# A GeGLU feed-forward kernel: ten blocks' first two products ahead instead of eight, x's first tokens loaded by halves of D, and two w_gate tiles kept in the result buffer

## The chip, the core and the metric

The kernel runs on one core of a Trainium2 chip. Five engines run their own instruction streams beside each other: TensorE (PE; its weight loads are PEld), VectorE (DVE), ScalarE (ACT), GpSimd (POOL) and SyncE (SP), which here only issues DMAs. The metric is the time of one execution on the device, in microseconds (us). A profile is one execution recorded by the hardware profiler; its span runs from the first to the last instruction of the program.

## The reference

`x` is 1024 tokens (32 x 32) by D = 1024, `w_gate` and `w_up` are 1024 x 3584, `w_down` is 3584 x 1024, all bf16.

```python
def _gelu(x):
    return jax.nn.gelu(x, approximate=True)

def reference(x, w_gate, w_up, w_down):
    return (_gelu(x @ w_gate) * (x @ w_up)) @ w_down
```

## The kernel before

Both stages are matrix products with one level of the Strassen-Winograd scheme: a product of 2 x 2 blocks is made with seven block products instead of eight, at the price of sums and differences of blocks. In the first stage the four blocks of the left side are the D halves of `w_gate` (a11 the first, a12 the second) and of `w_up` (a21, a22). The blocks of the right side are x transposed: B11 and B21 are the first and second D half of the first 512 tokens, B12 and B22 those of the other 512. The 3584 columns are cut into FT = 28 blocks of 128. One block product is four matmuls of 128 x 128 against 128 x 512, one for each 128 rows of a D half (KH = 4), accumulated in PSUM.

For each block i there are seven products. The first two, a11 x B11 and a12 x B21, are plain bf16 and need nothing but the loaded tiles (`first_products`, `second_products`; the matmuls are line 187). After the first, ScalarE copies the PSUM tile A to SBUF (E1, line 203); after the second it applies GELU to A (GL, line 210). The other five use sums: S1 to S4 of the weights, made by VectorE for blocks 0 and 1 and then by VectorE and GpSimd, and T1 to T4 of x, made once by VectorE (`t_sum`, line 158) from both halves of the tokens: T1 = B12 - B11, T2 = B22 - T1, T3 = B22 - B12, T4 = B21 - T2. `seed` (line 216) writes E1 back into PSUM as the start of a further sum.

The order of all instructions is written out by hand. The steps at the start are:

- Warm matmuls on a zeroed tile (line 137, NWARM = 18).
- SyncE issues the transposing DMA of x's first 512 tokens (xt0, line 135, 1 MB), then the pieces of the first w_gate tile (a tile holds two blocks' columns, 512 KB), tile 1, half of the first w_up tile, tiles 2 and 3, the transpose of the other 512 tokens (xt1, line 147), tile 4 and the rest of w_up. ScalarE issues one 128 KB piece of tile 0, after the fourth warm matmul.
- A lead of LEAD = 8 blocks: for each pair of blocks, two first products and two second products, 64 matmuls that need neither T1 to T4 nor S1 to S4.
- The further products of blocks 0 and 1, pairwise, mixed with the first products of blocks 8 and 9.
- A loop over i = 2 to 28 with the five further products of block i, and `ahead()`, which does the first product of the block `done` and the second of the one before. It is called in every iteration that is not in ALONE, until all blocks are done. A w_gate tile is loaded in every second iteration, into the one of five buffers (pool `gw`) that is free by then.

The four PSUM tiles that A and Y share (tag `q`) and the other four (tag `p`) are all of PSUM. E1 lies in a ring of four tiles, one for two blocks. The first stage's result goes to `gT` (28 blocks by 1024 tokens, bf16); the second stage multiplies it with `w_down` in the same scheme, and is left as it is.

Of the kernel before, what the change touches and what calls it, by code (L numbers as in the profile page):

```python
# [7 lines left out]
ACT = mybir.ActivationFunctionType  # L8
# [4 lines left out]
def kernel(  # L13
# [18 lines left out]
    nc = tc.nc  # L32
    P = nc.NUM_PARTITIONS
    fp32 = mybir.dt.float32
# [3 lines left out]
    xf = x.flatten_outer_dims()  # L38
    of = out.flatten_outer_dims()
    N, D = xf.shape  # L40
    F = w_gate.shape[1]
    NB = 512
    DT = D // P
    KH = DT // 2
    FT = F // P
# [1 line left out]
    DB = 512  # L47
    NDB = D // DB
    assert N == 2 * NB and DT % 2 == 0 and D % DB == 0 and FT % 4 == 0
    NWARM = 18  # L50
    LEAD = 8
    ALONE = (4, 7, 10, 13, 16, 19)
    KF = FT // 2
    TT = NT // 2
    JF = KF // 2
# [7 lines left out]
    ring = ctx.enter_context(tc.tile_pool(name="ring", bufs=RING))  # L63
# [2 lines left out]
    psum = ctx.enter_context(tc.tile_pool(name="ps", bufs=4, space=bass.MemoryType.PSUM))  # L66
    stage1 = ctx.enter_context(ExitStack())
    xpool = stage1.enter_context(tc.tile_pool(name="x", bufs=1))
    gw = stage1.enter_context(tc.tile_pool(name="gw", bufs=5))
    uw = stage1.enter_context(tc.tile_pool(name="uw", bufs=2))  # L70
    spool = stage1.enter_context(tc.tile_pool(name="s", bufs=2))
    epool = stage1.enter_context(tc.tile_pool(name="e", bufs=2))
# [1 line left out]
    gT = gpool.tile([P, FT, N], bf16, name="gT")  # L74
    xt0 = xpool.tile([P, DT, NB], bf16, name="xt0", tag="xt0")
    B11, B21 = xt0[:, :KH, :], xt0[:, KH:, :]
    xt1 = uw.tile([P, DT, NB], bf16, name="xt1", tag="uw")
    B12, B22 = xt1[:, :KH, :], xt1[:, KH:, :]
    WG, WU = {}, {}

    def load_gate(c, queue, lo=0, hi=DT):
        if c not in WG:
            WG[c] = gw.tile([P, DT, 2 * P], bf16, name="gw", tag="gw")
        queue.dma_start(
            out=WG[c][:, lo:hi, :], in_=wg_r[:, lo:hi, 2 * c * P : (2 * c + 2) * P]
        )

    def load_up(c, lo=0, hi=4):
        if c not in WU:
            WU[c] = uw.tile([P, DT, 4 * P], bf16, name="uw", tag="uw")  # L90
        nc.sync.dma_start(
            out=WU[c][:, :, lo * P : hi * P],
            in_=wu_r[:, :, (4 * c + lo) * P : (4 * c + hi) * P],
        )
# [4 lines left out]
    def a11(i):  # L99
        return block(WG, 2, i, 0)  # L100

    def a12(i):
        return block(WG, 2, i, 1)
# [4 lines left out]
    def a22(i):  # L108
        return block(WU, 4, i, 1)
# [12 lines left out]
    def psum_p(name):  # L122
        return psum.tile([P, NB], fp32, name=name, tag="p")

    def psum_q(name):
        return psum.tile([P, NB], fp32, name=name, tag="q")

    with tc.manual_schedule():
        zt = opool.tile([P, NB], bf16, name="zt", tag="o")
        nc.vector.memset(zt, 0.0)  # L130
        warm = [psum_p("warm") for _ in range(4)]
        table = opool.tile([P, 8], bf16, name="table", tag="o")
        nc.scalar.activation(table, zt[:, 0:8], ACT.Gelu_apprx_tanh)

        nc.sync.dma_start_transpose(out=xt0, in_=xf[0:NB, :])
        for n in range(NWARM):
            nc.tensor.matmul(warm[n % 4], lhsT=zt[:, 0:P], rhs=zt, start=True, stop=True)
            if n == 3:
                nc.scalar.activation(table, warm[n][:, 0:8], ACT.Copy)
                load_gate(0, nc.scalar, 0, 2)  # L140
        load_gate(0, nc.sync, 2, KH)
        load_gate(0, nc.sync, KH, DT)
        load_gate(1, nc.sync)
        load_up(0, 0, 2)
        load_gate(2, nc.sync)
        load_gate(3, nc.sync)
        nc.sync.dma_start_transpose(out=xt1, in_=xf[NB:N, :])
        load_gate(4, nc.sync)
        load_up(0, 2, 4)

        T = {}
# [3 lines left out]
        def t_sum(name, a, b, step=2):  # L155
            for k in range(0, KH, step):
                ks = slice(k, k + step)
                nc.vector.tensor_tensor(T[name][:, ks, :], a[:, ks, :], b[:, ks, :], ALU.subtract)
# [19 lines left out]
        def copy_a22(i):  # L178
            nc.scalar.activation(C22[i], a22(i), ACT.Copy)

        A, E1, GL = {}, {}, {}

        def pair_product(ps, lhs, rhs, first, cuts):
            for lo, hi in zip(cuts, cuts[1:]):
                for p, l in zip(ps, lhs):
                    for k in range(lo, hi):
                        nc.tensor.matmul(  # L187
                            p,
                            lhsT=l[:, k, :],
                            rhs=rhs[:, k, :],  # L190
                            start=(first and k == 0),
                            stop=(k == KH - 1),
                            skip_group_check=True,
                        )

        def first_products(*blocks, cuts=(0, KH)):
            for i in blocks:
                A[i] = psum_q("a")
            pair_product([A[i] for i in blocks], [a11(i) for i in blocks], B11, True, cuts)
            for i in blocks:  # L200
                if i % 2 == 0:
                    E1[i // 2] = ring.tile([P, 2, NB], fp32, name="e1", tag="ring")
                nc.scalar.activation(E1[i // 2][:, i % 2, :], A[i], ACT.Copy)  # L203

        def second_products(*blocks, cuts=(0, KH)):
            pair_product([A[i] for i in blocks], [a12(i) for i in blocks], B21, False, cuts)
            for i in blocks:
                if i % 2 == 0:
                    GL[i // 2] = half.tile([P, 2, NB], bf16, name="gl0", tag="half")
                nc.scalar.activation(GL[i // 2][:, i % 2, :], A[i], ACT.Gelu_apprx_tanh)  # L210
# [3 lines left out]
        def seed(i):  # L214
            X[i] = psum_p("x")
            nc.scalar.activation(X[i], E1[i // 2][:, i % 2, :], ACT.Copy)

        done = LEAD + 2

# [7 lines left out]
        def sixth_products(*blocks):  # L227
            cuts = range(0, KH + 1, 2)
            pair_product([X[i] for i in blocks], [S2[i] for i in blocks], T["T2"], False, cuts)
            for i in blocks:  # L230
                E2[i] = epool.tile([P, NB], fp32, name="e2", tag="e2")
                nc.scalar.activation(E2[i], X[i], ACT.Copy)
# [9 lines left out]
        def seventh_products(*blocks):  # L242
            cuts = range(0, KH + 1, 2)
            pair_product([X[i] for i in blocks], [S3[i] for i in blocks], T["T3"], False, cuts)
            for i in blocks:
                e3 = epool.tile([P, NB], fp32, name="e3", tag="e3")
                nc.scalar.activation(e3, X[i], ACT.Copy)  # L247
                U1[i] = epool.tile([P, NB], bf16, name="u1", tag="u1")
                nc.vector.tensor_tensor(U1[i], Y[i], e3, ALU.add)  # L249
# [16 lines left out]
        t_sum("T2", B22, T["T1"])  # L266
        t_sum("T3", B22, B12)
        t_sum("T4", B21, T["T2"])
        between = {2: lambda: copy_a22(0), 4: lambda: seed(0), 6: lambda: seed(1)}
        for n in range(0, LEAD, 2):  # L270
            first_products(n)
            first_products(n + 1)
            if n in between:
                between[n]()
            second_products(n)
            second_products(n + 1)
        for k in range(KH):
            nc.scalar.activation(T["B22"][:, k, :], B22[:, k, :], ACT.Copy)
        copy_a22(1)
# [2 lines left out]
        pair_product(  # L282
            [Y[0], Y[1]], [S1[0], S1[1]], T["T1"], True, range(KH + 1)
        )
        first_products(8)
        sixth_products(0, 1)
        first_products(9)
        seventh_products(0, 1)
        second_products(8)
        early_sums(2, nc.vector)  # L290
        second_sum(2)
        seed(2)
# [6 lines left out]
            third_product(i)  # L299
        copy_a22(2)  # L300
        finish(0)
        load_gate(5, nc.sync)
        load_up(1)

        for i in range(2, FT + 1):
            here, prev, more = i < FT, i - 1 if i > 2 else None, i + 1 < FT
            if more and i > 2:
                early_sums(i + 1)
            if here:
                sixth_products(i)  # L310
                if more:
                    seed(i + 1)
            if prev:
                fourth_product(prev)
            if more:
                second_sum(i + 1)
                late_sums(i + 1)
            if prev:
                finish(i - 2)
            if here:  # L320
                fifth_product(i)
            if here and i not in ALONE and done <= FT:
                ahead()
            if here:
                seventh_products(i)
                if more:
                    copy_a22(i + 1)
            if prev:
                third_product(prev)
            if here and i % 2 == 0:  # L330
                if i // 2 + 5 < FT // 2:
                    load_gate(i // 2 + 5, nc.sync)
                if i % 4 == 0 and i // 4 + 1 < FT // 4:
                    load_up(i // 4 + 1)
        finish(FT - 1)
# [37 lines left out]
        B11 = lambda j: V11[j // 2][:, two(j % 2), :]  # L373
        B12 = lambda j: V12[:, two(j), :]
        B21 = lambda j: V21[j]
# [149 lines left out]
```

## Time and profile before

| | |
|---|---|
| time, median of 3 runs | 277.34 us (276.94 to 277.44) |
| time of the profiled execution | 277.3 us |
| its span | 275.5 us |
| granted TensorE clock, mean | 1.000 |
| ACT busy | 137.9 us (50%) |
| read from HBM, written | 22.02 MB, 2.10 MB |

The times are us from the span's start. In the timeline a row gives the start, the length, the engine (SPq and ACTq are DMA issues), the line, the operation with output and inputs, the count of instructions merged into it, and in brackets the idle time before it and what ended it. The waits give who waited for whom, the total in us, how often, and the longest. Windows give for a stretch its length, then busy time and count of each engine, the granted clock, the DMA share and GB/s; with a line named, TensorE's matmuls and weight loads of that line alone. The DMA view of a stretch gives GB/s in 40 equal slices, the packets and bytes of the queues (q1 is SyncE's, q10 ScalarE's), and the DMAs issued in it with their size and the time from issue to landing.

### The profile page before, as it was taken

To read this page: it belongs to the slowest core of one execution; us is meant where nothing else is said; L and a number is where in the kernel's file an instruction comes from. 1 tells how busy PE (TensorE), PEld (TensorE's weight loads), DVE (VectorE), ACT (ScalarE), POOL (GpSimd) and SP (SyncE) were. 2 spreads that over 40 slices of the span, in tenths; PEclk is the share of its full clock that TensorE was granted. 3 is DMA by queue.
4 is the path that set the end of the run, shared out by engine and by line. 5 is a ranking of instruction groups with operands and counts; after the bars stand their busy time and mean duration, and the time that the engine had idled before them with its cause. 6 is when DMAs were issued, how large, how long until landed. Compare 5 with 4: busy or idle time off the path is not lost.

```text
span 275.5 us, 3345 instructions
## 1 busy us (share of the span) xinstructions
PE 270.1 (98%) x1194; PEld 190.3 (69%) x1194; DVE 188.9 (69%) x227; ACT 137.9 (50%) x237; POOL 87.0 (32%) x81
## 2 busy tenths in 40 slices
PE   7999999999999999999999999999999999999994
PEld 2446767777677776777766777764447888888883
DVE  0179965667666676666766555759994999999900
ACT  2578476666566565665656666541100072860311
POOL 0000374458544585455854444600000000000000
PEclk9999999999999999999999999999999999999999
DMA  8996420512152071161420120359702000000321
GB/s 187 293 259 177 152 76 0 176 57 76 37 191 79 0 229 46 34 187 43 155 76 21 55 76 4 101 184 330 225 0 77 2 0 0 0 2 0 114 77 38
DMA packets 40928, 26.42 MB, mean 96 GB/s; under 512 B 9168, under 2 KB 40912, under 8 KB 40912
## 3 DMA queue, kind: packets, MB, share of 16 engines
q1 hardware_dynamic: 40496, 25.96, 32.1%
q10 hardware_dynamic: 416, 0.26, 0.3%
q8 instruction: 9, 0.15, 0.2%
q14 instruction: 7, 0.06, 0.1%
HBM read 22.02 MB, written 2.10 MB: 88 GB/s over the span
## 4 chain that ended last, share of the span: by engine, by line
PE 96%; DMA 2%; ACT 0%; issue 0%
PE x L187 19%; PE x L380 18%; PE y L113 18%; PE a L187 18%; PE x L113 9%; PE y L380 9%; PE z L380 4%; DMA xt<-in_x_dram 2%; PE y L187 1%; ACT o_sb L492 0%
## 5 line engine op out<-in xcount | busy, mean ns | idle before, releaser
L187 PE MATMUL x<-T,s 128*128 128x512 f32 x224 | 63.8, 409 | 0.0
L187 PE MATMUL a<-xt,gw 128*128 128x512 bf16 x224 | 52.5, 380 | 0.8 <-DMA xt<-in_x_dram 0.8
L176 POOL TENSOR_TENSOR s<-gw,s 128x512 fp32r<-128x512 bf16 x26 | 30.6, 1179 | 60.0 <-PE y L113 59.3
L187 PEld LDWEIGHTS x<-T,s 128*128 128x128 f32 x224 | 41.9, 188 | 10.7
L249 DVE TENSOR_TENSOR u<-y,e 128x512 bf16<-128x512 f32 x28 | 19.3, 691 | 34.9 <-ACT e L247 34.3
L172 DVE TENSOR_TENSOR s<-s,gw 128x512 fp32r<-128x512 f32 x28 | 40.8, 1456 | 0.0
L187 PEld LDWEIGHTS <-gw 128*128 128x128 bf16 x224 | 20.0, 98 | 28.2 <-issue 5.9
L236 DVE TENSOR_TENSOR gT<-gl,x 128x512 bf16<-128x512 bf16 x28 | 19.2, 686 | 18.4 <-PE x L113 18.4
L256 ACT ACTIVATE gl<-h 128x512 bf16<-128x512 bf16 x28 | 17.7, 631 | 27.5 <-DVE h L254 27.5
L113 PE MATMUL x<-T,c 128*128 128x512 f32 x112 | 30.4, 393 | 0.0
L113 PE MATMUL y<-B,s 128*128 128x512 f32 x112 | 30.2, 391 | 0.0
L167 POOL TENSOR_TENSOR s<-uw 128x512 fp32r<-128x512 bf16 x25 | 29.1, 1164 | 0.0
L168 POOL TENSOR_TENSOR s<-gw,uw 128x512 fp32r<-128x512 bf16 x25 | 29.0, 1161 | 0.0
L203 ACT ACTIVATE e<-a 128x512 f32<-128x512 f32 x28 | 16.7, 597 | 22.5 <-PE a L187 22.4
L113 PE MATMUL y<-T,s 128*128 128x512 f32 x104 | 27.8, 389 | 0.0
L380 PE MATMUL x<-tc,sc 128*128 128x512 f32 x112 | 25.7, 389 | 0.0
L113 PEld LDWEIGHTS y<-B,s 128*128 128x128 f32 x112 | 21.0, 188 | 4.8
L113 PEld LDWEIGHTS x<-T,c 128*128 128x128 f32 x112 | 20.9, 188 | 4.8 <-ACT e L247 0.5
L380 PEld LDWEIGHTS x<-tc,sc 128*128 128x128 f32 x112 | 21.0, 188 | 4.4
L247 ACT ACTIVATE e<-x 128x512 f32<-128x512 f32 x28 | 16.7, 599 | 14.5 <-PE x L187 14.5
L113 PEld LDWEIGHTS y<-T,s 128*128 128x128 f32 x104 | 19.5, 188 | 4.1
L380 PEld LDWEIGHTS <-gT 128*128 128x128 bf16 x112 | 10.9, 98 | 13.3 <-issue 0.3
(52 smaller groups left out, 322.3 us busy)
## 6 DMA issues: line engine op xcount, KB each, us to landing
gw<-in_w_gate_dram SPq DMA_DIRECT2D x13, 512.0 KB, 4.0
uw<-in_w_up_dram SPq DMA_DIRECT2D x6, 1024.0 KB, 6.3
v<-in_w_down_dram SPq DMA_DIRECT2D x5, 512.0 KB, 3.3
v<-in_w_down_dram SPq DMA_DIRECT2D x4, 640.0 KB, 8.7
v<-in_w_down_dram SPq DMA_DIRECT2D x8, 256.0 KB, 4.6
out_dram<-o_sb SPq DMA_DIRECT2D x15, 128.0 KB, 1.7
uw<-in_w_up_dram SPq DMA_DIRECT2D x2, 512.0 KB, 5.9
gw<-in_w_gate_dram SPq DMA_DIRECT2D x1, 256.0 KB, 3.4
```

Of the source, the lines that this page charges most:

```text
L113: nc.tensor.matmul(ps, lhsT=lhs[:, k, :], rhs=rhs[:, k, :], start=(first and k == 0), stop=(k == KH - 1), skip_group_check=True,)
L167: engine.tensor_tensor(S1[i], a21(i), a22(i), ALU.add)
L168: engine.tensor_tensor(S3[i], a11(i), a21(i), ALU.subtract)
L172: nc.vector.tensor_tensor(S2[i], S1[i], a11(i), ALU.subtract)
L176: engine.tensor_tensor(S4[i], a12(i), S2[i], ALU.subtract)
L187: nc.tensor.matmul(p, lhsT=l[:, k, :], rhs=rhs[:, k, :], start=(first and k == 0), stop=(k == KH - 1), skip_group_check=True,)
L203: nc.scalar.activation(E1[i // 2][:, i % 2, :], A[i], ACT.Copy)
L236: nc.vector.tensor_tensor(gT[:, i, 0:NB], GL[i // 2][:, i % 2, :], X[i], ALU.mult)
L247: nc.scalar.activation(e3, X[i], ACT.Copy)
L249: nc.vector.tensor_tensor(U1[i], Y[i], e3, ALU.add)
L256: nc.scalar.activation(G1[i], h1, ACT.Gelu_apprx_tanh)
L380: nc.tensor.matmul(ps, lhsT=lhs[:, i, t * P : (t + 1) * P], rhs=rhs[:, i, :], start=(first and j == 0 and i == 0), stop=(last and j == JF ...
```

## The change

- The warm matmuls go from 18 to 11.
- x's first 512 tokens come in two transposing DMAs on SyncE, one for each D half (B11, then B21), 512 KB each.
- ScalarE issues three loads of 256 KB: the first D half of w_gate tile 0 as its first instruction, the first D half of tile 1 after the third warm matmul, the second D half of tile 0 after the eleventh. SyncE issues, behind the two transposes, the second D half of tile 1, tiles 2 and 3, half of w_up, tile 4, xt1, tile 5 and the rest of w_up.
- LEAD goes from 8 to 10. The first four blocks do their four first products and then their four second ones; the others go on in pairs. `seed(0)` and `seed(1)` come at blocks 4 and 6 as before, `copy_a22(0)` moves to block 8.
- ALONE gets 22 and 25, so that `ahead()` is called twice less in the loop.
- `gw` has four buffers instead of five. Tiles 4 and 5 are loaded into `gT`, into the places of the result's blocks 24 to 27, which are written at the end of the stage. In the loop, tile 7 is loaded in iteration 2, 8 in 4, 9 in 6, and 10 to 13 in 12 to 18.
- E1 of blocks 8 and 9 gets a tile of its own in the pool `x`.

```diff
-    NWARM = 18
-    LEAD = 8
-    ALONE = (4, 7, 10, 13, 16, 19)
+    NWARM = 11
+    LEAD = 10
+    ALONE = (4, 7, 10, 13, 16, 19, 22, 25)
...
-    gw = stage1.enter_context(tc.tile_pool(name="gw", bufs=5))
+    gw = stage1.enter_context(tc.tile_pool(name="gw", bufs=4))
...
+    for c in (4, 5):
+        WG[c] = gT[:, FT - 12 + 2 * c : FT - 10 + 2 * c, :].rearrange("p a (b f) -> p (a b) f", f=2 * P)
...
+        nc.sync.dma_start_transpose(out=B11, in_=xf[0:NB, 0 : KH * P])
+        load_gate(0, nc.scalar, 0, KH)
...
-        nc.sync.dma_start_transpose(out=xt0, in_=xf[0:NB, :])
         for n in range(NWARM):
             nc.tensor.matmul(warm[n % 4], lhsT=zt[:, 0:P], rhs=zt, start=True, stop=True)
-            if n == 3:
-                nc.scalar.activation(table, warm[n][:, 0:8], ACT.Copy)
-                load_gate(0, nc.scalar, 0, 2)
-        load_gate(0, nc.sync, 2, KH)
-        load_gate(0, nc.sync, KH, DT)
-        load_gate(1, nc.sync)
-        load_up(0, 0, 2)
+            if n in (2, NWARM - 1):
+                nc.scalar.activation(table, warm[n % 4][:, 0:8], ACT.Copy)
+                load_gate(int(n == 2), nc.scalar, *((0, KH) if n == 2 else (KH, DT)))
+        nc.sync.dma_start_transpose(out=B21, in_=xf[0:NB, KH * P : D])
+        load_gate(1, nc.sync, KH, DT)
         load_gate(2, nc.sync)
         load_gate(3, nc.sync)
+        load_up(0, 0, 2)
+        load_gate(4, nc.sync)
         nc.sync.dma_start_transpose(out=xt1, in_=xf[NB:N, :])
-        load_gate(4, nc.sync)
+        load_gate(5, nc.sync)
         load_up(0, 2, 4)
...
-                    E1[i // 2] = ring.tile([P, 2, NB], fp32, name="e1", tag="ring")
+                    pool, tag = (xpool, "e1") if i == LEAD - 2 else (ring, "ring")
+                    E1[i // 2] = pool.tile([P, 2, NB], fp32, name="e1", tag=tag)
...
-        between = {2: lambda: copy_a22(0), 4: lambda: seed(0), 6: lambda: seed(1)}
-        for n in range(0, LEAD, 2):
-            first_products(n)
-            first_products(n + 1)
-            if n in between:
-                between[n]()
-            second_products(n)
-            second_products(n + 1)
+        between = {4: lambda: seed(0), 6: lambda: seed(1), 8: lambda: copy_a22(0)}
+        for blocks in ((0, 1, 2, 3), (4, 5), (6, 7), (8, 9)):
+            for n in blocks:
+                first_products(n)
+            if blocks[0] in between:
+                between[blocks[0]]()
+            for n in blocks:
+                second_products(n)
...
-        first_products(8)
+        first_products(LEAD)
         sixth_products(0, 1)
-        first_products(9)
+        first_products(LEAD + 1)
         seventh_products(0, 1)
-        second_products(8)
+        second_products(LEAD)
...
-        load_gate(5, nc.sync)
+        load_gate(6, nc.sync)
...
-                if i // 2 + 5 < FT // 2:
-                    load_gate(i // 2 + 5, nc.sync)
+                c = i // 2 + (6 if i < 8 else 4)
+                if c in range(7, 10) and i < 8 or c in range(10, FT // 2):
+                    load_gate(c, nc.sync)
```

## The prediction

> Terms: the four halves that matter at the start are called B11 and B21 (the two D halves of the first 512 tokens, transposed), g0lo and g0hi (first and second D half of the w_gate tile of blocks 0 and 1), g1lo and g1hi (the same of blocks 2 and 3).
>
> **What bounds the kernel now.** I read the page first, then TensorE's waits, then TensorE's timeline at the start.
>
> ```profile
> span 275.5 us, 3345 instructions
> ...
> PE 270.1 (98%) x1194; PEld 190.3 (69%) x1194; DVE 188.9 (69%) x227; ACT 137.9 (50%) x237; POOL 87.0 (32%) x81
> ...
> PE 96%; DMA 2%; ACT 0%; issue 0%
> ```
>
> ```profile
> PE warm L137 <- DVE zt L130: 1.2, 1, 1.2
> PE a L187 <- DMA xt<-in_x_dram: 0.8, 1, 0.8
> ```
>
> ```profile
> 1.19 5.43 PE L137 MATMUL warm<-zt 128*128 128x512 bf16 x18 [1.19 <-DVE zt L130]
> 7.41 14.14 PE L187 MATMUL a<-xt,gw 128*128 128x512 bf16 x64 [0.79 <-DMA xt<-in_x_dram]
> 21.20 2.20 PE L187 MATMUL y<-T,s 128*128 128x512 f32 x8
> ```
>
> The page says that TensorE is busy 98% and makes up 96% of the chain. The waits say that it waits twice in the whole span: 1.2 us for the zeroed tile and 0.8 us for x. The timeline says that the first real matmul starts at 7.41 us; from there TensorE never waits until its last one. The change leaves the 1176 real matmuls as they are, so the time is the moment S at which real work starts (7.41) plus a constant, plus any new wait. The profiled execution took 277.3 us (span 275.5, and 1.8 around it), the median is 277.34: the sum goes against 277.3 and needs no correction. A real matmul of the lead takes (21.20 - 7.41)/64 = 0.2155 us.
>
> What S waits for is x's transpose, issued first on SyncE:
>
> ```profile
> 0.73 3.79 SPq L135 DMA_TRANSPOSE xt<-in_x_dram  x1
> ...
> 10.79 6.77 SPq L147 DMA_TRANSPOSE xt<-in_x_dram  x1
> ```
>
> ```profile
> DMA packets 4136, 1.07 MB, mean 272 GB/s; under 512 B 4076, under 2 KB 4136, under 8 KB 4136
> ...
> q1 hardware_dynamic: 4076, 1.04, 116.1%
> q10 hardware_dynamic: 60, 0.03, 2.6%
> ...
> xt<-in_x_dram SPq DMA_TRANSPOSE x1, 6.6
> ```
>
> The second fence is the DMA view from 2.1 to 6.05 us: the transpose's 256-byte packets (q1, SyncE's queue) fill it. It landed 6.6 us after its issue, at 7.37, and TensorE went on 0.04 later.
>
> **The change, part by part.** *Seven warm matmuls fewer.* The windows of the warm line show 7 matmuls at 0.413 us up to 4.08 and 12 at 0.21 after it:
>
> ```profile
> 1.19:4.08 2.89, 2.89 (x7) 1.04 (x8) 1.00 0.76 172
> 4.08:6.63 2.55, 2.54 (x12) 0.97 (x10) 1.00 1.25 292
> ```
>
> Eleven end at about 4.08 + 4 x 0.21 = 4.95 instead of 6.63. They cost nothing as long as x lands later than 4.95; that is the earliest possible S.
>
> *B11 alone first, g0lo beside it.* Full transpose rate is read from 4.1 to 5.8 us, that of plain loads from 6.9 to 8.4:
>
> ```profile
> DMA packets 1926, 0.49 MB, mean 290 GB/s; under 512 B 1926, under 2 KB 1926, under 8 KB 1926
> ```
>
> ```profile
> DMA packets 903, 0.45 MB, mean 299 GB/s; under 512 B 26, under 2 KB 903, under 8 KB 903
> ```
>
> A half transpose (524,288 bytes) takes 1.81 us, 256 KB of weights 0.88. ScalarE now issues g0lo as its first instruction, at 0.73 with B11; its table load slides 0.43 behind and still ends before the warm matmul that its next instruction waits for. The two move 2.69 us of data together; with the first packet at about 1.8 to 2.1 and a ramp of 0.25, B11's last packet comes at about 4.75. How long from last packet to landing? Two cases lie in the trace. The transpose of xt1 had no load of ScalarE behind it: packets until 19.1, landed 10.79 + 8.9 = 19.69, so 0.6. The first transpose had one waiting, and its landing came 1.3 after its last packets at 6.05:
>
> ```profile
> 3.19 0.43 ACTq L84 DMA_DIRECT2D gw<-in_w_gate_dram  x1
> ```
>
> ```profile
> q1 hardware_dynamic: 198, 0.05, 74.2%
> q10 hardware_dynamic: 89, 0.05, 51.6%
> ```
>
> ```profile
> q10 hardware_dynamic: 122, 0.06, 110.9%
> q1 hardware_dynamic: 8, 0.00, 4.5%
> ```
>
> These are the queues from 5.8 to 6.1 and from 6.1 to 6.3. The load issued at 3.19 moved nothing while the transpose had packets, and then its 256 packets ran through at once, ahead of SyncE's own loads issued from 4.59. I read this as: a load of ScalarE can't break into a transpose, but takes the engines when its packets end, before its landing is signalled. In the changed kernel g1lo, issued near 2.75 (after the third warm matmul), waits in just that place behind B11, with twice the packets. So the landing is 4.75 + 0.6 = 5.35 (no slip) up to 4.75 + 1.3 + 0.43 = 6.5 (slip of double size). I take 6.3, near the upper end, as its case is the nearer one. S = 6.3, bounds 5.35 and 6.5.
>
> Against this stands a rule of the Trainium skill, page "DMA: Bandwidth & Descriptors", section "Latency and other measured facts": a transpose whose middle dimension isn't contiguous runs at 261 GB/s. B11 takes 512 of 1024 columns of each row, so it might apply; no run here shows it. By that figure a half takes 2.01 us, an estimate, S would be 0.2 later and the sum below 276.4.
>
> *Four first products, then four second ones.* B21 and g0hi are needed 16 x 0.2155 = 3.45 after S, at 9.75. If g1lo goes in front (0.88), B21's packets run from 5.6 to 7.45; g0hi, issued when the eleventh warm matmul is done (5.25), runs 7.45 to 8.3 and lands about 8.9; B21 lands between 8.05 and 9.2. Slack 0.5. If instead g1lo runs behind B21 it lands at 7.9, but then B11 had no slip: blocks 2 and 3 start at 7.9 instead of 5.35 + 1.72 = 7.1, and the effective S is 6.15. Both orders give nearly the same S.
>
> *Later weights.* The second products of blocks 2 and 3 need g1hi at S + 5.2, the pairs after them tile 2 at S + 6.9, tile 3 at S + 10.3, tile 4 at S + 13.8 (11.5, 13.2, 16.6, 20.1). Behind g0hi at 8.3, with 0.88 for g1hi and 1.75 for each 512 KB, they land at about 9.8, 11.5, 13.3 and, behind the w_up half, 16.8. No wait.
>
> *Two more lead blocks against a later xt1.* The sums of the later products hang on xt1:
>
> ```profile
> 12.64 0.69 DVE L167 TENSOR_TENSOR s<-uw 128x512 fp32r<-128x512 bf16 x1 [11.51 <-DMA uw<-in_w_up_dram]
> ...
> 17.10 0.69 DVE L176 TENSOR_TENSOR s<-gw,s 128x512 fp32r<-128x512 bf16 x1
> 19.71 2.50 DVE L158 TENSOR_TENSOR T<-xt,xt 128x512 fp32r<-128x512 bf16 x4 [1.91 <-DMA xt<-in_x_dram]
> 22.12 2.35 DVE L158 TENSOR_TENSOR T<-xt,T 128x1024 fp32r<-128x1024 bf16 x2
> ```
>
> T1's fourth slice is ready at 22.2 and needed by the seventh matmul after 21.20, at 22.5: slack 0.3, that of T2's second part about as much. One more 512 KB tile now goes ahead of xt1, so it lands near 19.69 + 1.75 = 21.45. The first T1 product then can't start before 21.45 + 1.2 = 22.65; the ten lead blocks last 80 x 0.2155 = 17.24, so S below 5.4 gains nothing. The w_up half takes the place that tile 3 had, 3.5 us later (16.1); VectorE's eight early sums (5.15 us) end at 21.3, just ahead. At S = 6.3 both are hidden with 0.9 to spare. The two added blocks aren't added work: the main loop has two fewer (ALONE is longer).
>
> *Main loop.* With four buffers and two tiles in the result buffer the tightest load is that of tile 10, issued after iteration 12 and read in iteration 14. Before, a load stands at the same place:
>
> ```profile
> 97.02 0.37 SPq L84 DMA_DIRECT2D gw<-in_w_gate_dram  x1
> ```
>
> ```profile
> gw<-in_w_gate_dram SPq DMA_DIRECT2D x1, 512.0 KB, 4.0
> ```
>
> ```profile
> 102.88 1.90 PE L187 MATMUL a<-xt,gw 128*128 128x512 bf16 x8
> ```
>
> It lands at 101.0, 1.9 before the lead product of iteration 14: cost nothing. The moved copies of ScalarE and the extra sum tile find the same order of waits; half of ScalarE's time is idle.
>
> **Sum.** S from 7.41 to 6.3, no new wait: 277.3 - 1.1 = 276.2 us.
>
> **Rivals.** *Better:* no slip, and g1lo lands in time; then xt1 decides, S = 5.4 to 5.6, time 275.4. For it: 0.6 from packets to landing at xt1. Against: both loads of ScalarE can't be early.
>
> *No change:* transposes beside plain loads stall. From 14.4 to 19.2 us xt1's packets fell to a sixth of their rate while the tile ahead was still landing:
>
> ```profile
> GB/s 286 303 290 282 267 275 275 290 213 100 47 34 38 275 288 292 288 292 288 292 288 292 288 292 288 292 288 292 288 292 288 292 288 292 288 292 288 292 286 242
> ```
>
> Slices are 0.12 us; five of them at about 86 of 288 GB/s lose 0.42 us. Before, x's first transpose met nothing ahead of it. If B11 behind g0lo and B21 behind g1lo lose that each, on top of the upper bounds, B11 lands at 6.5 + 0.42 = 6.9 and B21 at 9.2 + 0.84 = 10.05, where it is needed at 10.4: S = 6.95, time 276.85.
>
> *Slower:* the queues are served in order of issue. Then g0hi, issued at 5.25, comes behind tile 2, which SyncE issues at about 5.1 (two half transposes of 1.9 and one load of 0.5 from 0.73). In order: g0lo and B11 to 4.75, B21 6.55, g1lo 7.45, g1hi 8.3, tile 2 10.05, g0hi 10.95, landed 11.55. The second product of block 0 waits for it, so S is in effect 11.55 - 3.45 = 8.1 and the time 278.0. It decides as soon as tile 2 goes ahead of g0hi. For it: the load of ScalarE did start in its place between SyncE's. Against: it ran before the first transpose was signalled.
>
> *The clock.* The warm matmuls run at half speed for 2.9 us, though the granted clock reads 1.00 in both rows. With 1.3 us idle after 4.95 (0.79 before) the slow stretch could come back or come late: 2.9 us at 0.413 does 7 matmuls where 13.5 would fit, 1.4 us lost, 277.6. The Trainium skill, page "TensorE: Matmul & The Clock Gate", Part 1, has a free-running window of about 3.4 us: one busy one releases the clock, one idle one throttles it again. By that rule 1.3 us idle isn't enough; the traced 0.79 us without a slow matmul behind it agrees as far as it goes.
>
> **How the numbers follow.** Forecast 276.2 (275.7 to 276.7): 0.50. Better, 275.4: 0.13. Transposes stall, 276.85: 0.18. In order, 278.0: 0.14. Clock, 277.6: 0.05. What a measurement tells from no change is 0.2%, 0.55 us: below 276.8 is faster, above 277.9 slower. Forecast and better are faster, a third of the stall case too: 0.68. Same: the rest of it, the clock, a mild in-order case: 0.20. Slower: 0.12. The range reaches down to 275.2, xt1's bound with the spread of the runs shown, and up to 277.9, short of the in-order case.
>
> **What would show it.** The first `a` product at about 6.3 with x named as the releaser; a wait of xt under 1.5 us; no wait of `a` for gw at the 9th and 17th matmul; the first y product of T1 17.3 us after S. In the DMA view, q10 packets between B11's and B21's. Wrong, if TensorE shows a second wait near 9.75 (in order), if the first `a` starts after 6.9, if the seventeenth to twentieth matmuls take 0.41, or if T1 or tile 10 is named as a releaser.

## The result, and the profile after

The changed kernel takes 276.71 us (276.27 to 277.12, 22 runs) against 277.35 (276.94 to 278.01, 22 runs) of the kernel before: ratio 0.9978, 95% interval 0.9971 to 0.9984. That is 0.64 us or 0.22% less. 276.2 was forecast, with a range from 275.2 to 277.9: the sign is right, the time lies in the range, and the gain is a little over half of the 1.1 us of the sum. The profiled execution has a span of 275.0 us (275.5 before).

The page of the changed kernel, its head and the chain:

```profile
span 275.0 us, 3348 instructions
...
PE 95%; DMA 3%; SPq 1%; ACT 0%; issue 0%
```

TensorE's waits in the whole span, which answer to the two shown of before:

```profile
PE warm L140 <- DVE zt L134: 1.2, 1, 1.2
PE a L190 <- DMA xt<-in_x_dram: 0.5, 1, 0.5
```

TensorE's timeline at the start:

```profile
1.19 4.88 PE L140 MATMUL warm<-zt 128*128 128x512 bf16 x11 [1.19 <-DVE zt L134]
6.14 3.91 PE L190 MATMUL a<-xt,gw 128*128 128x512 bf16 x16
10.57 10.52 PE L190 MATMUL a<-xt,gw 128*128 128x512 bf16 x48 [0.52 <-DMA xt<-in_x_dram]
20.92 3.62 PE L190 MATMUL a<-xt,gT 128*128 128x512 bf16 x16
24.19 2.19 PE L190 MATMUL y<-T,s 128*128 128x512 f32 x8
```

The wait for x has moved: it no longer stands before the first product (6.14) but before the 17th, the first that needs B21 (10.57). The first y product comes at 24.19. Before, it came at 21.20 with 16 lead products fewer, which is 21.20 + 3.45 = 24.65 on the same count: 0.46 us are gained by then. The rows give it as a sum: the start 7.41 - 6.14 = 1.27 gained; from 6.14 to 10.57 there are 4.43 us for 16 products that need 3.45, 0.98 lost; from 10.57 to 24.19 the other 64 take 13.62 instead of 13.79, 0.17 gained. The last 0.17 were a wait that I had overlooked. In the trace of before, TensorE's weight load shows tile 2 coming late:

```profile
14.46 6.59 PEld L187 LDWEIGHTS <-gw 128*128 128x128 bf16 x32 [0.48 <-DMA gw<-in_w_gate_dram]
```

Two matmuls there start 0.37 us apart instead of 0.2155, too short a pause for the profile to name as a wait of TensorE; "never waits" in the prediction was too strong.

The issues on SyncE and ScalarE after the change (an SPq or ACTq row lasts as long as its issuing engine was held):

```profile
0.74 1.42 SPq L131 DMA_TRANSPOSE xt<-in_x_dram  x1
2.21 4.95 SPq L144 DMA_TRANSPOSE xt<-in_x_dram  x1
7.21 1.75 SPq L86 DMA_DIRECT2D gw<-in_w_gate_dram  x3
```

```profile
0.74 0.42 ACTq L86 DMA_DIRECT2D gw<-in_w_gate_dram  x1
...
2.77 0.37 ACTq L86 DMA_DIRECT2D gw<-in_w_gate_dram  x1
...
6.18 0.37 ACTq L86 DMA_DIRECT2D gw<-in_w_gate_dram  x1
```

B11 landed 5.4 us after its issue, at 6.1, B21 8.2 after, at 10.4; 9.9 was needed. The DMA view of B21's own stretch, 6.2 to 8.4, and of 8.5 to 9.2:

```profile
GB/s 307 210 284 303 293 284 307 303 298 298 163 56 56 56 56 51 79 275 289 298 289 293 275 293 298 293 293 284 289 289 298 293 275 293 293 298 293 275 298 289
...
q1 hardware_dynamic: 1954, 0.50, 120.5%
q10 hardware_dynamic: 120, 0.05, 8.9%
...
xt<-in_x_dram SPq DMA_TRANSPOSE x1, 8.2
```

```profile
q10 hardware_dynamic: 418, 0.21, 114.2%
q1 hardware_dynamic: 22, 0.01, 3.5%
```

Two things are to be seen. Around 6.8 to 7.1 us the transpose falls to a fifth of its rate, while the last packets of g1lo (q10) are still out. And from 8.5 to 9.2, when all but 22 of B21's packets are through, it is ScalarE's third load (g0hi) that has the DMA engines; B21's landing is signalled only after it, 1.75 us after its last packet at 8.68.

### The profile page after: what moved, and what is told of

It is laid out like the page before. It is cut to its first block, busy times and chain, and to the rows that moved or that the text cites. A ratio compares the mean times of both kernels' runs of the same rounds, so it can differ in the third digit from the quotient of the medians.

```text
span 275.0 us, 3348 instructions
## 1 busy us (share of the span) xinstructions
PE 269.7 (98%) x1187; PEld 189.9 (69%) x1187; DVE 189.1 (69%) x227; ACT 138.1 (50%) x238; POOL 87.1 (32%) x81
## 4 chain that ended last, share of the span: by engine, by line
PE 95%; DMA 3%; SPq 1%; ACT 0%; issue 0%
PE x L190 19%; PE x L385 18%; PE y L115 18%; PE a L190 16%; PE x L115 9%; PE y L385 9%; PE z L385 4%; DMA xt<-in_x_dram 3%; PE y L190 1%; SPq L131 1%; ACT o_sb L497 0%
## 5 line engine op out<-in xcount | busy, mean ns | idle before, releaser
L190 PE MATMUL a<-xt,gw 128*128 128x512 bf16 x192 | 45.0, 382 | 0.6 <-DMA xt<-in_x_dram 0.5
L179 POOL TENSOR_TENSOR s<-gw,s 128x512 fp32r<-128x512 bf16 x22 | 26.0, 1180 | 48.4 <-PE y L115 47.7
L190 PEld LDWEIGHTS <-gw 128*128 128x128 bf16 x192 | 17.5, 98 | 24.7 <-issue 5.7
L175 DVE TENSOR_TENSOR s<-s,gw 128x512 fp32r<-128x512 f32 x24 | 34.5, 1437 | 0.0
L171 POOL TENSOR_TENSOR s<-gw,uw 128x512 fp32r<-128x512 bf16 x21 | 24.4, 1161 | 0.0
L214 ACT ACTIVATE gl<-a 128x512 bf16<-128x512 f32 x28 | 16.7, 596 | 6.8 <-PE a L190 6.5
```

The source lines that it names most:

```text
L171: engine.tensor_tensor(S3[i], a11(i), a21(i), ALU.subtract)
L175: nc.vector.tensor_tensor(S2[i], S1[i], a11(i), ALU.subtract)
L179: engine.tensor_tensor(S4[i], a12(i), S2[i], ALU.subtract)
L190: nc.tensor.matmul(p, lhsT=l[:, k, :], rhs=rhs[:, k, :], start=(first and k == 0), stop=(k == KH - 1), skip_group_check=True,)
```

## The experiments

The times of a run are set against the kernel before on the same chip. My theory after the result: B21's landing is what is left of the loss, and g0hi behind it makes it late. The rivals: the transposes themselves are late; the warm matmuls set the start; the split or the lead does nothing.

**The load behind B21 moved to SyncE.**

```diff
-            if n in (2, NWARM - 1):
+            if n == 2:
...
-                load_gate(int(n == 2), nc.scalar, *((0, KH) if n == 2 else (KH, DT)))
+                load_gate(1, nc.scalar, 0, KH)
         nc.sync.dma_start_transpose(out=B21, in_=xf[0:NB, KH * P : D])
+        load_gate(0, nc.sync, KH, DT)
```

> The second D half of w_gate tile 0 is issued by SyncE right behind B21 instead of by ScalarE after the last warm matmul. Theory (slip): in the changed kernel B21's packets end at 8.5 us, but its landing is signalled only at 10.43, because ScalarE's load takes the DMA engines between B21's packets and its end mark. Without a load of ScalarE there, B21 lands near 9.3, tile 0's second half near 10.1, TensorE's wait before the 17th matmul shrinks from 0.52 to about 0.1, and the time is 276.3. Rival (the transposes themselves are late): B21 still lands at about 10.4 and the time stays 276.7.

Measured: ratio 1.0002 (0.9991 to 1.0012). The DMA view gives B21 7.0 us from its issue at 2.21, so it landed at 9.2, and TensorE now waits for w_gate:

```profile
PE warm L140 <- DVE zt L134: 1.2, 1, 1.2
PE a L191 <- DMA gw<-in_w_gate_dram: 0.7, 1, 0.7
PE a L191 <- DMA xt<-in_x_dram: 0.4, 1, 0.4
```

The theory's landing came (9.3 expected, 10.4 by the rival), its time did not. SyncE was held by B21's issue until 7.16, so g0hi was issued at 7.21; its issue to landing took 3.6 us (10.8), and between 8.3 and 9.2 the queue moved little, the packets under 512 B still being B21's and its end marks:

```profile
DMA packets 403, 0.13 MB, mean 148 GB/s; under 512 B 253, under 2 KB 403, under 8 KB 403
```

B21's packets ended where they had, at 8.69, and it landed 0.53 after them. The 17th product still started 0.9 us later than it could have, now for g0hi. In this profile another 0.3 us stands at the start, where the edit changes nothing: B11 landed at 6.42. In the eight traces that start with the same two issues it lands anywhere from 5.98 to 6.42, so a difference of that size between two traces says nothing. My reading is that g0hi belongs on ScalarE, which is free, but not where it is ready just as B21 ends.

**The same with 7 warm matmuls** (NWARM = 7).

> As e1_g0hi_sync, but with 7 warm matmuls instead of 11. In the profile of the changed kernel all 11 ran at 0.427 us and ended at 6.1, when B11 landed too (6.09). Theory (the landing sets the start): the first product still starts at 6.1 and the time is that of e1_g0hi_sync within 0.15. Rival (the warm matmuls set the start): the first product starts below 5.9 and the time falls by 0.2 or more. Third possibility (the slow stretch ends later with fewer warm matmuls): the first 4 to 10 products take 0.43 each and the time rises by 0.4 to 1.4.

Measured: 1.001 (0.9998 to 1.0022). The first product came at 6.27 all the same: B11's landing sets the start. But the third possibility came too, in another form. Windows from the first product on (TensorE's busy time and count first, the granted clock in the third column from the end; a matmul on a window's edge counts in both):

```profile
6.27:7.37 1.10, 1.10 (x6) 0.50 (x6) 0.00 (x0) 0.04 (x1) 0.00 (x0) 1.00 1.27 250
7.37:10.78 3.41, 3.41 (x10) 1.21 (x9) 0.00 (x0) 1.39 (x3) 0.00 (x0) 0.50 0.98 247
10.78:14.00 3.22, 3.22 (x17) 1.45 (x16) 0.00 (x0) 2.16 (x4) 0.00 (x0) 1.00 1.12 307
```

The first products start 0.2155 us apart, so the seven warm matmuls had been enough to bring the clock up. Then, from 7.37 to 10.78, it stands at half, and the matmuls start 0.427 us apart: TensorE had been idle for 2.05 us before 6.27. There is no wait for B21 (landed at 9.2), yet the first y product is at 25.03 against 24.46 with 11 warm ones.

**Only the lead undone.**

```diff
-    LEAD = 10
-    ALONE = (4, 7, 10, 13, 16, 19, 22, 25)
+    LEAD = 8
+    ALONE = (4, 7, 10, 13, 16, 19)
...
-        load_gate(4, nc.sync)
         nc.sync.dma_start_transpose(out=xt1, in_=xf[NB:N, :])
+        load_gate(4, nc.sync)
...
```

> Only the longer lead is undone: 8 blocks ahead, the old ALONE, xt1 again ahead of tile 4; split x, queues and warm matmuls stay as changed. Theory: xt1 lands near 20.0, the first T1 product can't start before 21.2, while the lead ends at 6.14 + 0.52 + 64 x 0.2155 = 20.45, so 0.7 of the gain is lost: 277.3 to 277.4, and VectorE's T1 is named as what the y products wait for. Rival (the two added blocks are worth nothing): 276.7 and no wait at T1.

Measured: 1.0048 (1.0036 to 1.006), 0.7% (1.9 us) above the changed kernel's ratio; I had expected 0.7 us. TensorE's waits name T1, and VectorE's timeline shows why:

```profile
PE a L190 <- DMA xt<-in_x_dram: 1.5, 2, 1.1
PE y L190 <- DVE T L161: 1.2, 1, 1.2
```

```profile
16.18 0.69 DVE L170 TENSOR_TENSOR s<-uw 128x512 fp32r<-128x512 bf16 x1 [15.04 <-DMA uw<-in_w_up_dram]
...
20.64 0.69 DVE L179 TENSOR_TENSOR s<-gw,s 128x512 fp32r<-128x512 bf16 x1
21.25 2.49 DVE L161 TENSOR_TENSOR T<-xt,xt 128x512 fp32r<-128x512 bf16 x4
```

xt1 had landed at 10.47 + 9.1 = 19.6; T1 waited 1.7 us more for VectorE, whose eight early sums could start only when w_up landed (16.2), because w_up now stands behind tiles 2 and 3. TensorE came to the first y product at about 20.6 (10.23 + 48 x 0.2155) and got T1's first slice at 22.0. The remaining slices came slower than TensorE used them, too. So the 1.9 us are the price of the shorter lead with this order of loads; a shorter lead with w_up in its old place was not run.

**Only the split undone**: one transpose of xt0, the rest as changed.

> Only the split of x's first transpose is undone: one transposing DMA of 1 MB, everything else as changed. Theory (the gain is the earlier start on B11): the whole lands at about 8.0 (0.9 for ScalarE's first load, 3.6 for the transpose, 0.8 to 1.3 to landing), TensorE starts there and doesn't wait again, time 277.8, 1.0 above the changed kernel. Rival (the second half is what counts, the split gives nothing): TensorE starts near 7.1, time 276.7.

Measured: 1.0117 (1.0104 to 1.013), 3.9 us above the changed kernel instead of 1.0. The DMA issue and TensorE's timeline:

```profile
xt<-in_x_dram SPq DMA_TRANSPOSE x1, 8.6
```

```profile
1.19 4.51 PE L140 MATMUL warm<-zt 128*128 128x512 bf16 x11 [1.19 <-DVE zt L134]
9.39 15.26 PE L189 MATMUL a<-xt,gw 128*128 128x512 bf16 x63 [3.69 <-DMA xt<-in_x_dram]
```

x landed at 9.3, not 8.0. All but 11 of its packets were through by 7.2, the last at 7.6; from 7.2 to 8.1 the queue of ScalarE moved 434 of 445 packets, beginning with those of a load issued at 2.77. It is the same as behind B21, with 1.8 us from the last packet to landing. On top, 3.7 us of idle TensorE brought the slow clock back (0.53 granted from 9.39 to 12.18). So this run shows that a whole x behind these early loads is worse than the halves, but its 3.9 us do not price the split by itself.

**g0hi on ScalarE, but ahead of B21's packets.**

```diff
-            if n in (2, NWARM - 1):
+            if n == 2:
...
-                load_gate(int(n == 2), nc.scalar, *((0, KH) if n == 2 else (KH, DT)))
+                load_gate(1, nc.scalar, 0, KH)
+                load_gate(0, nc.scalar, KH, DT)
```

> As the changed kernel, but ScalarE issues the second D half of tile 0 straight after the first half of tile 1 (about 3.1 us), not after the last warm matmul. Theory (a load of ScalarE that is ready when a transpose's packets end runs before its landing is signalled): now both loads run after B11, before B21's packets, and none is ready at B21's end; B21's packets end near 9.2 and it lands 0.6 to 0.9 later, at 9.8 to 10.1, so TensorE's wait of 0.52 falls to 0.3 or less and the time to 0.996 of the kernel before. Rival (only the bytes ahead of B21 count): B21 moves 0.9 later with the load ahead of it, lands near 11.2, and the time is that of the kernel before or more.

Measured: 0.9959 (0.9947 to 0.9971). The waits, and from the DMA view the stretch 8.4 to 9.3 with B21's landing:

```profile
PE warm L140 <- DVE zt L134: 1.2, 1, 1.2
PE a L191 <- DMA xt<-in_x_dram: 0.3, 1, 0.3
```

```profile
DMA packets 1031, 0.26 MB, mean 289 GB/s; under 512 B 1018, under 2 KB 1031, under 8 KB 1031
```

```profile
xt<-in_x_dram SPq DMA_TRANSPOSE x1, 7.7
```

B21's packets now run until 9.33, 0.65 later than in the changed kernel, and it lands at 9.87, 0.56 earlier: 0.54 from the last packet to landing instead of 1.75. For the landing the theory holds against the rival that only the bytes ahead count. Of the time it explains a part: the first y product is at 23.63, 0.56 earlier than in the changed kernel, and only 0.24 of that is the shorter wait. Another 0.3 is that here the first 16 products ran at full speed from the start (3.61 us instead of 3.91).

**All early loads on SyncE**, in the order B11, g0lo, g1lo, g0hi, B21, with 10 warm matmuls.

> All early loads on SyncE in one order: B11, first half of tile 0, first half of tile 1, second half of tile 0, B21, then as changed; no load of ScalarE, 10 warm matmuls. Theory: B11's packets are not mixed with a load, end near 4.0 and it lands near 4.8; tile 0's half lands near 5.6 and TensorE starts there; B21 lands near 9.3 with 0.2 of wait; if the clock is up by then, the time is 0.9 below the changed kernel, 0.9945 of the kernel before. Rival (the mix of queues is needed, SyncE's issue is the limit): loads issued behind one another on SyncE start with gaps as in e1_g0hi_sync, the first product starts at 6.2 or later, and the time is 0.9975 or more.

Measured: 0.9987 (0.9969 to 1.0006). This is what the rival had said (0.9975 or more, a first product at 6.2 or later), not the 0.9945 of the theory. B11 landed at 4.9 as the theory had it, but the first product waited 1.3 us for g0lo and started at 6.74:

```profile
PE a L189 <- DMA gw<-in_w_gate_dram: 1.3, 1, 1.3
```

g0lo took 4.5 us from its issue at 2.21 to 6.7. It stood behind a transpose on one queue, and started late and slowly: from 4 to 5 us, where B11's packets end and g0lo's begin, the mean rate was 223 GB/s. No wait for B21 is named in this run.

**The kernel before without ScalarE's load** (its 128 KB are issued by SyncE behind x).

> The kernel before, with ScalarE's 128 KB load issued by SyncE behind x instead (one load of 256 KB). Theory (slip): x's transpose, whose packets end at 6.05, now lands at 6.6 to 6.9 instead of 7.37; the first product waits for w_gate instead, near 7.6. Rival (the landing of a first transpose is late anyway): x lands at 7.3 to 7.4 again.

There is one time only (277.76), so no interval. x landed at 6.5 instead of 7.4:

```profile
xt<-in_x_dram SPq DMA_TRANSPOSE x1, 5.8
```

From x's last packet to its landing it is 0.49 us here, 1.21 in the kernel before: in that kernel, too, the load of ScalarE behind the transpose cost its landing 0.7 us. The first product starts only at 8.06, as the 18 warm matmuls ran slow until 7.2 in this profile and w_gate, issued at 4.46, landed at 8.0.

**Only the lead** (x whole, queues, pairs and 18 warm matmuls as before).

> Only the lead of ten blocks, with the tiles in the result buffer; x whole, queues, pairs and 18 warm matmuls as before. Theory (the lead only keeps an earlier start from being lost at T1, and adds no gain of its own): the first product at 7.4, no wait after it, time within 0.1% of the kernel before. Rival (the lead itself shortens the path): 0.998 or less.

Measured: 0.9997 (0.9988 to 1.0005). The first product is at 7.40, nothing waits after it. The lead alone gives nothing; without it the earlier start is lost.

**18 warm matmuls with g0hi early.**

> As e5_g0hi_early, with 18 warm matmuls as before instead of 11. Theory (B11 lands near 6.1, and warm matmuls that still run then push the start back): 18 end at 6.6 where the clock is up at 4.1, at 8.9 where it isn't up until then; the first product starts at 6.7 to 8.9 and the time is 0.3 to 1.0 above e5_g0hi_early. Rival (B21 and later loads decide, the warm matmuls don't matter): the same time within 0.1%.

Measured: 1.0005 (0.9995 to 1.0015), 0.41% or 1.1 us above the same kernel with 11 on the same chip (e11 below). The first product is at 6.85 (6.02 with 11 there, 6.11 in e5), as the theory said. The time rose a little more than its 0.3 to 1.0. TensorE also waits 0.3 for T1 in this profile, as xt1 landed at 23.7, 1.4 later than in e5. The trace shows an accident that fits: 15 of xt1's 16 landing signals had come by 22.2, the last at 23.7, and in the DMA view from 13 to 24 us a packet of 16 KB stands that e5's does not have. It took 1.0 us from 21.62 on, just as xt1's last packets went.

```profile
q8 instruction: 1, 0.02, 0.6%
```

That is one trace; the times of this run go from 276.91 to 278.28.

**The changed kernel and the one with g0hi early, side by side.**

> The changed kernel itself, on the same chip as the two beside it: 0.9975 to 0.9985 of the kernel before, with B21's landing after 10.2 and a wait of 0.3 to 0.6 before the 17th product.

> The kernel of e5_g0hi_early once more, beside the changed one: if moving the second half of tile 0 ahead of B21 is worth what its profile says (the wait from 0.52 to 0.28), it is 0.1% to 0.2% below the changed kernel, 0.9955 to 0.997 of the kernel before. If the first result was a lucky chip, it is 0.9975 or more.

Measured: changed 0.9972 (0.9963 to 0.9981), a little below what I had expected, with B21 8.3 after its issue and a wait of 0.6 before the 17th product; g0hi early 0.9964 (0.9951 to 0.9977), B21 8.1 after its issue. The waits of g0hi early:

```profile
PE a L191 <- ACT e L208: 0.7, 1, 0.7
PE a L191 <- DMA xt<-in_x_dram: 0.2, 1, 0.2
```

The 0.7 stand before the 17th product, at 10.42. The profile names a copy of ScalarE, but in e5 the same product started before that copy had ended, so it is B21, which landed at 10.3. In this profile B21's packets ran beside a slow tail of ScalarE's loads from 7.2 to 8.3. They ended at 9.66 and the landing came 0.62 later, without the slip; but the wait did not fall to 0.28. It is longer than the changed kernel's, and what its first y product is earlier by (24.04 against 24.25) comes from an earlier start and faster first products. So the slip is gone in both traces of g0hi early, while what that is worth in time is not shown: g0hi early beats the kernel before beyond doubt, and side by side with the changed kernel it is 0.08% lower, with intervals that overlap.

## Why the prediction was right, and where its size was off

**Start.** Forecast 6.3, measured 6.14. The number is right by luck, as two errors cancel. I had B11's packets end at 4.75 and its landing pushed back to 6.3 by g1lo. In the trace B11's last packet is at 5.55, because its packets were mixed with g0lo's from 2.75 to 3.7 and stalled (which I had only in a rival). A load of ScalarE that is ahead does share the engines with a transpose, which I had not allowed for. And B11 landed 0.54 after that packet, with no slip at all, though g1lo was ready and ran right behind it, ahead of B21.

**Warm matmuls.** They were to end at 4.95, worked out from a clock that had come up at 4.08 in the trace of before. All eleven ran slow here and ended at 6.07, just when B11 landed. The clock came up after that: 16 products took 3.91 us where 3.61 is what they take in e5, so 0.3 was lost. It is the clock rival in a small form, 0.3 for the 1.4 that I had priced. The 4.08 was one draw: the first warm matmul starts at 1.19 in all 13 traces, and by their clock records the step up comes anywhere from 4.0 to 7.2 (at 4.1 in e3, which has the same eleven).

**B21.** This is the term that was mis-sized: "B21 lands between 8.05 and 9.2. Slack 0.5." It landed at 10.4, 0.5 late. The 1.2 beyond the upper end are all in its packets, whose last went at 8.68, not 7.45: B11's ended 0.8 later, g1lo took from 5.3 to 6.9 instead of 0.88, and the transpose stalled beside its tail. The landing came 1.75 after the last packet, just what the worst case had. So "no new wait" in the sum failed: the 17th product started 0.68 later than it could have. A second wait near 9.75 was one of the prediction's own signs of being wrong; it came, from 10.05 on, though not by the order of issue that was named for it. With the 0.3 of the slow products that makes the 0.98 lost of the 1.27 gained, and with the 0.17 at tile 2 what is left is 0.46 in the profile, 0.64 in the medians.

**The slip.** The reading of the first trace, that a load of ScalarE takes the engines before a transpose's landing is signalled, is shown: the slip goes when the load is taken away, in e7 and, behind B21, in e1, e5 and e11. All traces together say the same. From the last packet to landing it is 0.46 to 0.62 us for 28 transposes. It is 1.21 and 1.25 for x in the kernel before and in e8, with 128 KB of ScalarE behind it, and 1.74 to 1.76 for B21 in the changed kernel, e10 and e3 and for the whole x in e4, with 256 KB. (The one left, xt1 in e9, is told there.) It did not hit B11, where g1lo was ready too, in eight traces. What makes the difference is open; in the six cases that slip, no further transpose stood next on SyncE's queue.

**Later weights, xt1, main loop.** No wait named, as forecast; first y at 24.19, 18.05 after the start. That the lead covers xt1 is shown by e3 and e8 together, though in e3 it was the w_up half and VectorE's sums that bound, and not xt1's landing itself.

**Rivals.** In order of issue: refuted, since g1lo, issued at 2.77, ran before B21, issued at 2.21. (Its case did not arise either: SyncE was held until 7.16, so tile 2 was issued after g0hi.) Transposes stall: true in part, about 0.3 us at B21. That rival's time, 276.85, is nearer to the measured 276.71 than the 276.2 of the forecast, though not by its way: it had the start at 6.95 and no wait for B21. The rule of the Trainium skill, page "DMA: Bandwidth & Descriptors", section "Latency and other measured facts" (261 GB/s for a transpose of a non-contiguous middle dimension) does not show here: a half transpose undisturbed ran at 289 GB/s (8.4 to 9.3 in e5_g0hi_early), the whole one at 290.

## What to carry to other kernels

Splitting the first load lets the main engine start on half of it, but the gain is the earlier start less what the second half then comes late; work out both landings. A small load on another queue isn't free beside a large one: look in the DMA view at which queue moves packets between the large one's last packet and its landing, and issue the small one so that it is not ready just as the large one ends. A lead that only covers later loads is worth nothing by itself (e8) and everything with the earlier start (e3): test it both ways. And a landing or a clock step read from one trace is one draw: compare the traces of several runs before building 0.3 us on it.

## What the runs showed of the hardware that I had not expected

- The warm matmuls' slow stretch ends at a moment that the program does not set. They run back to back from 1.19 us, 0.427 us apart, and come to 0.2155 at 4.0 us in before, 4.9 in e8 and 7.2 in e7, all with 18 of them, and at 4.1 in e3 and 6.8 in the changed kernel. The granted clock reads 1.00 through this stretch all the same: each trace's clock records begin only with the step up.
- Idle time brought a second slow stretch, with 0.50 granted for 3.41 us: from 7.37 to 10.78 in e2, after 2.05 us of idle, and from 8.62 to 12.03 in e4, after 3.7. In e3, 1.14 us of idle brought none. The Trainium skill, page "TensorE: Matmul & The Clock Gate", Part 1, has a free-running window of about 3.4 us; the two stretches of 3.41 us agree with it. By its rule, as the prediction quotes it, an idle window throttles; in e2 the 3.4 us before the step down held only 2.05 us of idle, and the measurement decides.
- A transposing DMA holds SyncE: B21's issue took 4.95 us (3.79 for twice the bytes, issued alone at the start of before), and the loads behind it were issued only after it, from 7.21.
- Beside the tail of a plain load a transpose ran at 51 to 79 GB/s instead of 290.
